# Float64 weight words to float32: two ScalarE passes and three VectorE passes in place of one and six

## The chip, the cores and the metric

The kernel runs on one core of one Trainium2 chip. The metric is the device time of one execution in microseconds. Engines: TensorE (PE, with PEld for its weight loads), VectorE (DVE), ScalarE (ACT), GpSimd (POOL) and SyncE (SP), which issues most DMAs.

## What is computed

Chunked attention, then a mixer. q, k and v have the shape (8, 8, 576, 64) in float32. In each chunk of 64 positions:

```python
scores = scale * np.matmul(q_c, k_c.transpose(0, 1, 2, 4, 3))
scores = scores - np.max(scores, axis=-1, keepdims=True)
attn = np.exp(scores)
attn = attn / (np.sum(attn, axis=-1, keepdims=True) + 1e-09)
out = np.matmul(attn, v_c)
```

With x of shape (8, 576, 512) made from the heads, the mixer is

```python
xt = x.transpose(0, 2, 1)
h = xt @ U @ V
u = x + h.transpose(0, 2, 1)
ch = np.maximum(u @ w_ch1, 0.0) @ w_ch2
return (u + ch).astype(np.float32)
```

U (576 x 32), V (32 x 576), w_ch1 (512 x 2048) and w_ch2 (2048 x 512) arrive as float64, since each is a float32 array times a float64 scalar. [...]

## The kernel before, in words

**Work.** Batches go in pairs; a pair is nine tiles of 128 positions (three groups of three). A tile's attention: q and k are transposed on TensorE (ps_qT, ps_kT) and copied by ScalarE, TensorE makes scores (sc), VectorE takes maxima and subtracts (mx, ex), ScalarE exponentiates (ex, L415), TensorE transposes (ps_eT), ScalarE copies (eT), TensorE multiplies by the values (av), VectorE divides (sm, x). A batch's x goes through U (xh and xl are its high and low parts, y, ys) and V (u), is added to x, transposed (ut) and split (uth, utl). Every float32 operand of a large product is split into a high part in float32r, which ScalarE casts, and a low part, which VectorE subtracts; a product is three matmuls. For each of 16 slices f of the hidden width, h (L567, 12 matmuls) is made, relu gives hh (ScalarE) and hl (VectorE), and o (L593, 9 matmuls for three tiles) is added up. Weights are read once, for the first pair, and stay.

**Weights.** A tile Wf holds 1024 values (512 of w_ch1, 512 of w_ch2) for each of 128 partitions. `w_ops` loads its raw words (wraw, stride two between high words and between low words), `rounding` makes float32 of them in wroom, `splitting` makes w: `high` is a ScalarE cast (L308), `low` a VectorE subtraction (L311). W13 to W15 are converted in halves. U (320 values) and V (144) go through the same `rounding`; V then makes a round trip through DRAM (vrows, vall) to be spread, and ScalarE's cast L256 and VectorE's L261 put it into vst.

**Conversion before.** ScalarE takes the absolute value of the high word as float32, times 2^16 (L86). VectorE: clamp (L92); shift left 4 and right 1, which drops the sign and makes room (L93); join the sign bit of the high word (L96); keep the exponent alone, into the high word (L99); multiply the low word by 2^-52 and that power of two (L100); add (L101).

**Order.** For the first pair the code makes a list of `Op`s, each with an engine, an estimated time, what it comes after, and what it takes and frees of the buffers. `order` runs through them as a planner with a clock of its own: of what can start next on an engine within 0.05 us it picks the lowest rank, and that fixes the order of every engine's instructions, DMA issues included. On the chip each engine then works in this order, and waits where something is late. `LEAD` gives the ranks of the first stage (tiles T, projections P, mixes M, U, V, W), `STRETCHES` the blocks of h, relu and o; TensorE's h has the lowest claim. `turn` chains the conversions: one begins after a given step of the one before. The later pairs have an order that is written out by hand and is not touched.

Of the kernel before, what the change touches and what calls it, by code (L numbers as in the profile page):

```python
# [10 lines left out]
F32 = mybir.dt.float32  # L11
F32R = mybir.dt.float32r
U32 = mybir.dt.uint32
AF = mybir.ActivationFunctionType
ALU = mybir.AluOpType
# [6 lines left out]
def kernel(  # L22
# [11 lines left out]
    nc = tc.nc  # L34
# [46 lines left out]

    def magnitude(raw, a):
        af = a.bitcast(F32)
        nc.scalar.activation(af, raw[..., 1].bitcast(F32), AF.Abs, scale=2.0**16)  # L86

    def as_f32(raw, a):
        hi, lo = raw[..., 1], raw[..., 0]
        af, hf = a.bitcast(F32), hi.bitcast(F32)  # L90
        return [
            lambda: nc.vector.tensor_scalar(af, af, HI_MIN, HI_MAX, op0=ALU.max, op1=ALU.min),  # L92
            lambda: nc.vector.tensor_scalar(  # L93
                a, a, 4, 1, op0=ALU.logical_shift_left, op1=ALU.logical_shift_right
            ),
            lambda: nc.vector.scalar_tensor_tensor(  # L96
                a, hi, 0x80000000, a, op0=ALU.bitwise_and, op1=ALU.bitwise_or
            ),
            lambda: nc.vector.tensor_scalar(hi, a, 0xFF800000, None, op0=ALU.bitwise_and),  # L99
            lambda: nc.vector.scalar_tensor_tensor(hf, lo, 2.0**-52, hf, op0=ALU.mult, op1=ALU.mult),  # L100
            lambda: nc.vector.tensor_add(af, af, hf),  # L101
        ]

    def wslot(shape, dtype, name):
        return wpool.tile([P, *shape], dtype, tag="w", name=name, bufs=NF)
# [68 lines left out]
    turn = [None]  # L174

    def rounding(raw, room, after, take, n):

        st = {}
        k = n / 1024

        def begin():
            st["a"] = room()
            magnitude(raw, st["a"])
            st["steps"] = as_f32(raw, st["a"])

        o = Op("ACT", 0.2 + 0.95 * k, begin, after, turn[0], take=take)
        for z in range(6):
            us = 0.15 + 0.54 * k if z in (0, 1, 3) else 0.15 + 1.07 * k
            o = Op("DVE", us, lambda z=z: st["steps"][z](), o)
            if z == 2:  # L190
                turn[0] = o
        return o, st

    def splitting(st, high, low, after, free, n):
        k = n / 1024
        h = Op("ACT", 0.2 + 0.85 * k, lambda: high(st["a"].bitcast(F32)), *after)
        return Op("DVE", 0.15 + 1.07 * k, lambda: low(st["a"].bitcast(F32)), h, free=free)

    def conversion(raw, room, high, low, after, take, free, n):
        o, st = rounding(raw, room, after, take, n)  # L200
        return splitting(st, high, low, [o], free, n)
# [30 lines left out]
    def v_ops():  # L232
# [29 lines left out]

        ld = Op("SP", 1.0, load, take="w", lat=2.0)
        o, _ = rounding(Later(lambda: st["raw"]), room, ld, "w", n)
        o = Op("SP", 0.6, join, o, free="w w", lat=2.5)
        o = Op("SP", 0.9, spread, o, take="w", lat=2.5)
# [13 lines left out]
    def w_ops(f, after=None):  # L280
# [15 lines left out]
        for z in range(n):  # L296
            cols = slice(z * size, (z + 1) * size)

            def room(z=z):
                return wslot((size,), U32, f"wroom_{f}") if n == 1 else slot(U32, f"wroom_{f}_{z}")  # L300

            def high(v, cols=cols):
                if cols.start == 0:
                    del st["raw"]
                    w = st["w"] = wslot((2, 2 * DM), F32R, f"w_{f}")
                    w1[f] = w[:, :, 0:DM].rearrange("p s (c f) -> p s c f", c=NCC)
                    w2[f] = w[:, :, DM:]
                nc.scalar.copy(st["w"][:, 0, cols], v)  # L308

            def low(v, cols=cols):  # L310
                nc.vector.tensor_sub(st["w"][:, 1, cols], v, st["w"][:, 0, cols])  # L311

            raw = Later(lambda cols=cols: st["raw"][:, cols])
            tag = "w" if n == 1 else "slot"
            halves.append((*rounding(raw, room, ld, tag, size), high, low, tag))
        rounded = [h[0] for h in halves]
        return [splitting(r, high, low, rounded, tag, size) for _, r, high, low, tag in halves]


# [337 lines left out]
    for item in LEAD.split():  # L657
        rank[0] += 1
        z, i = item[0], int(item[1:] or 0)
# [145 lines left out]
```

## Time and profile before

| | |
|---|---|
| runs, us | 1030.47, 1030.82, 1032.12 |
| median, us | 1030.82 |
| profiled execution, span, us | 1032.0 (the times have no figure of their own for it; the highest run is 0.12 us longer) |
| mean granted clock of TensorE | 0.929 |
| HBM read and written | 45.83 MB, 9.51 MB |

The page cuts the span into 40 slices of 25.8 us. A row of a timeline has the start, the duration, the engine, the line, the operation with output and input, the count, and in brackets the idle time before it with what ended it. A row of groups has the count, the busy time and the mean of one in ns, and behind the bar the idle time before. A row of windows has the stretch, then the busy time of PE, PEld, DVE, ACT and POOL with counts, then the granted clock, the DMA share and GB/s. Of a name such as wraw the buffer's number is left out in the profile.

### The profile page before, as it was taken

How to read it: one execution, taken by the hardware profiler on the slowest of the kernel's cores; microseconds unless marked ns; L12 is line 12 of the kernel's file. 1: busy time of each engine (PE TensorE's matmuls, PEld its weight loads, DVE VectorE, ACT ScalarE, POOL GpSimd, SP SyncE). 2: the span in 40 equal slices, each digit the busy share in tenths (PEclk: the TensorE clock that was granted, in tenths of full speed). 3: DMA queues.
4: the chain of work that ended last, by engine and by line, in shares of the span. 5: the costliest groups of instructions: out<-in, count | busy, mean ns of one | idle time of the engine just before them, and what ended most of it. 6: DMA issues, size and time to landing. Idle time of an engine off the chain costs nothing.

```text
span 1032.0 us, 16637 instructions
## 1 busy us (share of the span) xinstructions
PE 980.7 (95%) x7032; PEld 862.0 (84%) x7032; DVE 419.5 (41%) x834; ACT 260.8 (25%) x467; POOL 26.4 (3%) x78
## 2 busy tenths in 40 slices
PE   5486999999999999999999999999999999999998
PEld 4364888888888888988888888988888889999997
DVE  3498999973333342322423242322333332211211
ACT  3453234322322222222222222222222231111110
POOL 7100000000000000000000000000000000000000
PEclk9667899999999999999999999999999999999999
DMA  9952142305121211021021210111121000000000
GB/s 187 217 184 88 42 113 82 103 34 129 34 63 31 63 31 32 34 55 37 32 62 32 62 32 10 53 34 43 48 53 41 31 1 1 31 1 1 31 1 30
DMA packets 123157, 56.40 MB, mean 55 GB/s; under 512 B 107276, under 2 KB 115724, under 8 KB 123084
## 3 DMA queue, kind: packets, MB, share of 16 engines
q1 hardware_dynamic: 121932, 52.99, 20.1%
q0 software_dynamic: 1152, 2.36, 1.2%
q8 instruction: 55, 0.90, 0.4%
q14 instruction: 18, 0.15, 0.0%
HBM read 45.83 MB, written 9.51 MB: 54 GB/s over the span
## 4 chain that ended last, share of the span: by engine, by line
PE 69%; DVE 0%; ACT 0%; DVEq 0%; issue 0%; ACTq 0%
PE h L567 30%; PE o L593 30%; PE av L424 1%; PE sc L393 1%; PE ut L535 1%; PE ps_eT L375 1%; PE ps_kT L375 1%; PE ps_qT L375 1%; PE u L523 1%; PE y L496 1%; PE y L495 1%; DVE x L605 0%; DVE ex L411 0%; ACT ex L415 0%; DVEq L800 0%; DVE mx L407 0%
## 5 line engine op out<-in xcount | busy, mean ns | idle before, releaser
L567 PE MATMUL h<-uth,w 128*128 128x384 f32 x1536 | 427.1, 342 | 4.9 <-ACT w L308 2.1
L593 PE MATMUL o<-w,hh 128*128 128x512 f32 x1152 | 364.3, 403 | 0.6 <-ACT hh L575 0.6
L567 PEld LDWEIGHTS h<-uth,w 128*128 128x128 f32 x1536 | 282.4, 189 | 13.8 <-ACT w L308 2.6
L580 DVE SCALAR_TENSOR_TENSOR hl<-h,hh 128x384 fp32r<-128x384 f32 x192 | 106.8, 556 | 430.4 <-ACT hh L575 430.4
L567 PE MATMUL h<-utl,w 128*128 128x384 f32 x768 | 260.2, 339 | 0.4 <-DVE utl L548 0.4
L593 PEld LDWEIGHTS o<-w,hh 128*128 128x128 f32 x1152 | 207.8, 189 | 35.8 <-ACT hh L575 0.9
L593 PE MATMUL o<-w,hl 128*128 128x512 f32 x576 | 217.9, 395 | 0.0
L575 ACT ACTIVATE hh<-h 128x384 fp32r<-128x384 f32 x192 | 94.3, 491 | 477.3 <-PE h L567 477.2
L567 PEld LDWEIGHTS h<-utl,w 128*128 128x128 f32 x768 | 144.9, 189 | 6.6 <-DVE utl L548 0.6
L593 PEld LDWEIGHTS o<-w,hl 128*128 128x128 f32 x576 | 108.2, 188 | 25.0 <-DVE hl L580 0.3
L375 PE MATMUL ps_eT<-ident,ex 128*128 128x128 f32 x144 | 24.8, 301 | 25.0 <-ACT ex L415 25.0
L415 ACT ACTIVATE ex<-ex 128x512 f32<-128x512 f32 x36 | 22.7, 632 | 89.7 <-DVE ex L411 89.1
L375 PEld LDWEIGHTS ps_eT<-ident,ex 128*128 128x128 f32 x144 | 18.9, 153 | 31.1 <-ACT ex L415 27.9
L407 DVE TENSOR_REDUCE mx<-sc 128x4 f32<-128x256 f32 x72 | 28.0, 418 | 37.7 <-PE sc L393 37.7
L488 DVE TENSOR_TENSOR xl<-x,xh 128x512 fp32r<-128x512 f32 x40 | 27.2, 687 | 29.6 <-ACT xh L484 25.6
L529 DVE TENSOR_TENSOR x<-u,x 128x512 f32<-128x512 f32 x36 | 24.1, 684 | 26.7 <-PE u L523 26.4
L548 DVE TENSOR_TENSOR utl<-ut,uth 128x512 fp32r<-128x512 f32 x36 | 24.5, 690 | 25.2 <-ACT uth L543 25.1
L605 DVE TENSOR_TENSOR x<-o,x 128x512 f32<-128x512 f32 x48 | 31.2, 685 | 7.7 <-PE o L593 7.6
L543 ACT CAST uth<-ut 128x512 fp32r<-128x512 f32 x36 | 20.9, 587 | 40.4 <-PE ut L535 36.6
L385 ACT COPY eT<-ps_eT 128x512 f32<-128x512 f32 x36 | 21.1, 586 | 39.4 <-PE ps_eT L375 39.4
L484 ACT CAST xh<-x 128x512 fp32r<-128x512 f32 x40 | 24.1, 621 | 17.8 <-PE y L496 7.5
L411 DVE TENSOR_TENSOR ex<-sc,mx 128x256 f32<-128x256 f32 x72 | 28.0, 417 | 0.8
(74 smaller groups left out, 590.2 us busy)
## 6 DMA issues: line engine op xcount, KB each, us to landing
wraw<-in_moe_w_ch_dram SPq DMA_DIRECT2D x32, 512.0 KB, 4.5
out_dram<-x SPq DMA_DIRECT2D x36, 256.0 KB, 2.1
vn<-in_v_dram SPq DMA_DIRECT2D x108, 64.0 KB, 2.9
qn<-in_q_dram SPq DMA_DIRECT2D x24, 256.0 KB, 3.3
kn<-in_k_dram SPq DMA_DIRECT2D x24, 256.0 KB, 4.1
qkv<-in_v_dram POOLq DMA_DIRECT2D x36, 64.0 KB, 6.3
qkv<-in_q_dram SPq DMA_DIRECT2D x8, 256.0 KB, 9.4
qkv<-in_k_dram SPq DMA_DIRECT2D x8, 256.0 KB, 7.6
```

The costliest lines, as they stand in the source:

```text
L375: nc.tensor.transpose(ps[:, j * P : (j + 1) * P], src[:, j * P : (j + 1) * P], ident)
L407: nc.vector.reduce_max(mx, st["sc"][e], axis=AX.X)
L411: nc.vector.tensor_sub(st["ex"][:, :, e, :], st["sc"][e], mx.unsqueeze(2).broadcast_to([P, HP, C]))
L484: nc.scalar.copy(st["h"], x_of[pr, i + 4 * e])
L488: nc.vector.tensor_sub(st["l"], x_of[pr, i + 4 * e], st["h"])
L529: nc.vector.tensor_add(x, st["u"], x)
L548: nc.vector.tensor_sub(ul[:, :, js], st["t"].rearrange("p (c t) -> p c t", c=NCC), uh[:, :, js])
L567: nc.tensor.matmul(ps[:, :GN], lhsT=w[:, z, cc], rhs=u[:, cc, :], start=(n == 0), stop=(n == 3 * NCC - 1))
L575: nc.scalar.activation(hh, ps[:, :GN], AF.Relu)
L580: nc.vector.scalar_tensor_tensor(hl, ps[:, :GN], 0.0, hh, op0=ALU.max, op1=ALU.subtract)
L593: nc.tensor.matmul(acc[j], lhsT=h[:, js], rhs=w2[f][:, z], start=(first and i == 0), stop=(final and i == 2),)
L605: nc.vector.tensor_add(x, ps, x)
```

## The change

`as_f32` now has three VectorE steps. The clamp stays (its line is 96 now). ScalarE gets a second pass, `low_bits` (line 90): the low word, as an integer, times 0.9375 x 2^-29 x (1 - 2^-10), in place and back to an integer, so that three bits of it remain, rounded. VectorE ors the high word's sign into it (line 97), then shifts the clamped word left by 3 and ors the low word in (line 100). The result is joined from bits, where before it was added from two floats. `rounding` makes the plan of these: the second pass `b` comes after the first on ScalarE, the sign join waits for both, and the next conversion may begin after the clamp (`turn`), where it was the third VectorE step. Every line behind moves down by 7.

```diff
+    LOW_STEP = 0.9375 * 2.0**-29 * (1.0 - 2.0**-10)
+
     def magnitude(raw, a):
-        af = a.bitcast(F32)
-        nc.scalar.activation(af, raw[..., 1].bitcast(F32), AF.Abs, scale=2.0**16)
+        nc.scalar.activation(a.bitcast(F32), raw[..., 1].bitcast(F32), AF.Abs, scale=2.0**16)
+
+    def low_bits(raw):
+        nc.scalar.activation(raw[..., 0], raw[..., 0], AF.Copy, scale=LOW_STEP)
...
             lambda: nc.vector.tensor_scalar(af, af, HI_MIN, HI_MAX, op0=ALU.max, op1=ALU.min),
-            lambda: nc.vector.tensor_scalar(
-                a, a, 4, 1, op0=ALU.logical_shift_left, op1=ALU.logical_shift_right
+            lambda: nc.vector.scalar_tensor_tensor(
+                lo, hi, 0x80000000, lo, op0=ALU.bitwise_and, op1=ALU.bitwise_or
             ),
             lambda: nc.vector.scalar_tensor_tensor(
-                a, hi, 0x80000000, a, op0=ALU.bitwise_and, op1=ALU.bitwise_or
+                a, a, 3, lo, op0=ALU.logical_shift_left, op1=ALU.bitwise_or
             ),
-            lambda: nc.vector.tensor_scalar(hi, a, 0xFF800000, None, op0=ALU.bitwise_and),
-            lambda: nc.vector.scalar_tensor_tensor(hf, lo, 2.0**-52, hf, op0=ALU.mult, op1=ALU.mult),
-            lambda: nc.vector.tensor_add(af, af, hf),
         ]
...
         o = Op("ACT", 0.2 + 0.95 * k, begin, after, turn[0], take=take)
-        for z in range(6):
-            us = 0.15 + 0.54 * k if z in (0, 1, 3) else 0.15 + 1.07 * k
-            o = Op("DVE", us, lambda z=z: st["steps"][z](), o)
-            if z == 2:
-                turn[0] = o
+        b = Op("ACT", 0.2 + 0.95 * k, lambda: low_bits(raw_of(raw)), o)
+        o = Op("DVE", 0.15 + 0.54 * k, lambda: st["steps"][0](), o)
+        turn[0] = o
+        o = Op("DVE", 0.15 + 1.07 * k, lambda: st["steps"][1](), o, b)
+        o = Op("DVE", 0.15 + 1.07 * k, lambda: st["steps"][2](), o)
         return o, st
```

Since the planner's times and chains change, the order moves on all engines in the first pair. SyncE's DMA issues are the same up to the loads of the second pair's first tile. Three places follow; wraw_249 is W0, wraw_346 and wraw_347 are W1, wraw_517 is W2, and the number behind a name is a buffer's.

ScalarE around V's cast (vst), before:

```order
L385 COPY eT_3_475<-ps_eT_3_445 128x512
L256 CAST vst<-vall 128x576
L484 CAST xh_0_3_526<-x_3_520 128x512
L415 ACTIVATE ex_4_501<-ex_4_501 128x512
L385 COPY qkT_5_542<-ps_qT_5_528 128x512
L385 COPY qkT_5_542<-ps_kT_5_535 128x512
L385 COPY eT_4_557<-ps_eT_4_544 128x512
L86 ACTIVATE wroom_583<-wraw_347 128x1024
```

and now:

```order
L392 COPY eT_3_472<-ps_eT_3_444 128x512
L87 ACTIVATE wroom_480<-wraw_346 128x1024
L90 ACTIVATE wraw_346<-wraw_346 128x1024
L422 ACTIVATE ex_4_500<-ex_4_500 128x512
L263 CAST vst<-vall 128x576
L491 CAST xh_0_3_533<-x_3_523 128x512
L392 COPY eT_4_540<-ps_eT_4_528 128x512
L392 COPY qkT_5_553<-ps_qT_5_535 128x512
```

W1's passes and the exponential of tile 4 have moved ahead of the cast that waits for V, and the eT copy of tile 4 ahead of tile 5's copies.

VectorE at the same place, W0's steps, before:

```order
L261 TENSOR_TENSOR vst<-vall,vst 32x576
L488 TENSOR_TENSOR xl_0_3_540<-x_3_520,xh_0_3_526 128x512
L93 TENSOR_SCALAR wroom_410<-wroom_410 128x1024
L96 SCALAR_TENSOR_TENSOR wroom_410<-wraw_249,wroom_410 128x1024
L99 TENSOR_SCALAR wraw_249<-wroom_410 128x1024
L100 SCALAR_TENSOR_TENSOR wraw_249<-wraw_249 128x1024
```

and now:

```order
L97 SCALAR_TENSOR_TENSOR wraw_249<-wraw_249 128x1024
L495 TENSOR_TENSOR xl_0_3_542<-x_3_523,xh_0_3_533 128x512
L268 TENSOR_TENSOR vst<-vall,vst 32x576
L100 SCALAR_TENSOR_TENSOR wroom_406<-wroom_406,wraw_249 128x1024
L443 TENSOR_SCALAR sm_4_582<-av_0_4_556 128x4
```

The first of W0's two joins stands ahead of vst, the second right behind it.

VectorE ahead of the exponential of tile 8, before:

```order
L605 TENSOR_TENSOR x_2_437<-o_2_914,x_2_437 128x512
L442 TENSOR_TENSOR x_7_951<-av_0_7_926,sm_7_947 128x4x64
L100 SCALAR_TENSOR_TENSOR wraw_517<-wraw_517 128x1024
L101 TENSOR_TENSOR wroom_710<-wroom_710,wraw_517 128x1024
L407 TENSOR_REDUCE mx_8_964<-sc_0_8_888 128x4
L411 TENSOR_TENSOR ex_8_963<-sc_0_8_888,mx_8_964 128x4x64
L407 TENSOR_REDUCE mx_8_964<-sc_0_8_889 128x4
L311 TENSOR_TENSOR w_966<-wroom_710,w_966 128x1024
L411 TENSOR_TENSOR ex_8_963<-sc_0_8_889,mx_8_964 128x4x64
```

and now:

```order
L612 TENSOR_TENSOR x_0_261<-o_0_887,x_0_261 128x512
L612 TENSOR_TENSOR x_1_336<-o_1_906,x_1_336 128x512
L612 TENSOR_TENSOR x_2_433<-o_2_915,x_2_433 128x512
L449 TENSOR_TENSOR x_7_960<-av_0_7_924,sm_7_947 128x4x64
L449 TENSOR_TENSOR x_7_960<-av_0_7_925,sm_7_947 128x4x64
L418 TENSOR_TENSOR ex_8_919<-sc_0_8_869,mx_8_920 128x4x64
```

W2's last passes and three of tile 8's four steps have moved ahead of the adds of o.

More of the change, by code (lines that the diff above doesn't have):

```diff
@@ L80 @@
     w2 = {}
+    LOW_STEP = 0.9375 * 2.0**-29 * (1.0 - 2.0**-10)
     def magnitude(raw, a):
-        af = a.bitcast(F32)
-        nc.scalar.activation(af, raw[..., 1].bitcast(F32), AF.Abs, scale=2.0**16)
+        nc.scalar.activation(a.bitcast(F32), raw[..., 1].bitcast(F32), AF.Abs, scale=2.0**16)
+    def low_bits(raw):
+        nc.scalar.activation(raw[..., 0], raw[..., 0], AF.Copy, scale=LOW_STEP)
     def as_f32(raw, a):
         hi, lo = raw[..., 1], raw[..., 0]
-        af, hf = a.bitcast(F32), hi.bitcast(F32)
+        af = a.bitcast(F32)
         return [
             lambda: nc.vector.tensor_scalar(af, af, HI_MIN, HI_MAX, op0=ALU.max, op1=ALU.min),
-            lambda: nc.vector.tensor_scalar(
-                a, a, 4, 1, op0=ALU.logical_shift_left, op1=ALU.logical_shift_right
+            lambda: nc.vector.scalar_tensor_tensor(
+                lo, hi, 0x80000000, lo, op0=ALU.bitwise_and, op1=ALU.bitwise_or
             ),
             lambda: nc.vector.scalar_tensor_tensor(
-                a, hi, 0x80000000, a, op0=ALU.bitwise_and, op1=ALU.bitwise_or
+                a, a, 3, lo, op0=ALU.logical_shift_left, op1=ALU.bitwise_or
             ),
-            lambda: nc.vector.tensor_scalar(hi, a, 0xFF800000, None, op0=ALU.bitwise_and),
-            lambda: nc.vector.scalar_tensor_tensor(hf, lo, 2.0**-52, hf, op0=ALU.mult, op1=ALU.mult),
-            lambda: nc.vector.tensor_add(af, af, hf),
         ]
@@ L197, in splitting, with raw_of @@
         return Op("DVE", 0.15 + 1.07 * k, lambda: low(st["a"].bitcast(F32)), h, free=free)
+    def raw_of(raw):
+        return raw.get() if isinstance(raw, Later) else raw
     def conversion(raw, room, high, low, after, take, free, n):
```

## The prediction

> **What bounds the kernel now.** I read the page first: busy shares, and the 40 slices (25.8 us each) for where TensorE is not busy.
>
> ```profile
> PE 980.7 (95%) x7032; PEld 862.0 (84%) x7032; DVE 419.5 (41%) x834; ACT 260.8 (25%) x467; POOL 26.4 (3%) x78
> PE   5486999999999999999999999999999999999998
> DVE  3498999973333342322423242322333332211211
> PEclk9667899999999999999999999999999999999999
> ```
>
> TensorE is busy for 980.7 of 1032.0 us, so 51.3 us are idle, and the row of slices puts nearly all of them into the first four slices, where the granted clock is low too. VectorE's row has its nines in slices 4 to 7, so it is full where TensorE is not. From the fifth slice on, only TensorE's own work counts, and the change leaves that alone. So I asked the chain of waits for TensorE over the first 150 us, and then its timeline for the places.
>
> ```profile
> PE ps_eT L375 <- ACT ex L415: 24.5, 3, 10.4
> PE u L523 <- DVE ys L506: 3.0, 2, 1.6
> ...
> 49.96 1.12 PE L375 MATMUL ps_eT<-ident,ex 128*128 128x128 f32 x4 [10.45 <-ACT ex L415]
> 59.81 1.65 PE L523 MATMUL u<-ys,vst 128*128 128x512 f32 x3 [1.62 <-DVE ys L506]
> 72.23 0.45 PE L567 MATMUL h<-uth,w 128*128 128x384 f32 x1 [1.67 <-ACT w L308]
> 73.49 1.01 PE L567 MATMUL h<-uth,w 128*128 128x384 f32 x2 [0.63 <-DVE w L311]
> 92.14 1.12 PE L375 MATMUL ps_eT<-ident,ex 128*128 128x128 f32 x4 [6.90 <-ACT ex L415]
> 146.14 0.44 PE L567 MATMUL h<-uth,w 128*128 128x384 f32 x1 [0.46 <-ACT w L308]
> 147.52 0.61 PE L567 MATMUL h<-uth,w 128*128 128x384 f32 x2 [0.76 <-DVE w L311]
> ```
>
> The reader sees five places. The first (10.45 us) and a similar one of 7 us near 22 us are not VectorE's: ScalarE itself stood still there for V's float64 words and for their way through DRAM.
>
> ```profile
> 28.05 0.33 ACT L86 ACTIVATE vroom<-vraw 128x144 f32<-128x144 f32 x1 [7.60 <-DMA vraw<-in_moe_V_dram]
> 48.18 0.67 ACT L256 CAST vst<-vall 128x576 fp32r<-128x576 f32 x1 [11.61 <-DMA vall<-vrows]
> ```
>
> The queue of SyncE is the same in both kernels beyond these transfers, so both landings stay: up to 48.18 us I credit nothing. The other places wait on conversions of weights that VectorE does in order with the attention's small steps.
>
> **The change part by part.** The price of one of each pass, from the groups kept apart by shape, first 130 us:
>
> ```profile
> L86 ACT ACTIVATE wroom<-wraw 128x1024 f32<-128x1024 f32 x7 | 8.1, 1152 | 0.0
> L100 DVE SCALAR_TENSOR_TENSOR wraw<-wraw 128x1024 f32<-128x1024 uint32 x6 | 7.3, 1221 | 0.1
> L96 DVE SCALAR_TENSOR_TENSOR wroom<-wraw,wroom 128x1024 uint32<-128x1024 uint32 x6 | 7.3, 1220 | 0.1
> L101 DVE TENSOR_TENSOR wroom<-wroom,wraw 128x1024 f32<-128x1024 f32 x6 | 7.3, 1220 | 0.1
> L308 ACT CAST w<-wroom 128x1024 fp32r<-128x1024 f32 x6 | 6.3, 1051 | 8.4 <-DVE wroom L101 8.4
> L92 DVE TENSOR_SCALAR wroom<-wroom 128x1024 f32<-128x1024 f32 x7 | 5.0, 712 | 0.0
> L93 DVE TENSOR_SCALAR wroom<-wroom 128x1024 uint32<-128x1024 uint32 x7 | 4.8, 690 | 0.1
> L99 DVE TENSOR_SCALAR wraw<-wroom 128x1024 uint32<-128x1024 uint32 x6 | 4.1, 689 | 0.1
> ```
>
> A weight tile costs VectorE 0.71 + 0.69 + 1.22 + 0.69 + 1.22 + 1.22 = 5.75 us before, and 0.71 + 1.22 + 1.22 = 3.15 us now, if the two new joins cost what the two old scalar_tensor_tensor rows cost; they read and write the same strided words as L96 and L100. That is 2.6 us less for each of 16 tiles, 41.6 us in all. It buys time only at the places above. ScalarE pays one more pass. The trace has none that writes uint32 at stride two; nearest are L86 (1152 ns, strided read) and L308 (1051 ns). I take 1.15 us; the floor is 1.05, and I set the ceiling at twice L86, 2.3 us, for a strided read and write together. Over 16 tiles that is about 18 us (17 to 37) on an engine that is busy 25% of the time.
>
> The Trainium skill, page "ScalarE: Activation LUTs", section "Rules for kernel authors", speaks against such a move: it says to run multiplications on VectorE, not on ScalarE. By instruction the rows agree (1152 ns against 689 to 712 for a VectorE pass over one tensor), and the sum over busy time would be a loss by that rule; the sum below goes by who waits.
>
> Place by place, with TensorE's own times:
>
> *u at 59.81.* Between V's arrival and ys, VectorE runs without a break.
>
> ```profile
> 48.89 0.75 DVE L261 TENSOR_TENSOR vst<-vall,vst 32x576 fp32r<-32x576 f32 x1 [8.91 <-ACT vst L256]
> ...
> 51.86 1.22 PE L424 MATMUL av<-qkv,eT 64*64 64x65 f32 x31
> ...
> 55.30 1.21 DVE L101 TENSOR_TENSOR wroom<-wroom,wraw 128x1024 f32<-128x1024 f32 x1
> ...
> 59.07 0.68 DVE L506 TENSOR_TENSOR ys<-y,ys 32x512 fp32r<-32x512 f32 x1
> ```
>
> From L93 to L101 (ending at 56.5) five passes of tile W0 stand there: 0.69 + 1.22 + 0.69 + 1.22 + 1.22 = 5.04 us. In the new order the sign join stands ahead of vst, in the 8.91 us in which VectorE idles, so one pass of 1.22 remains: 3.8 us less. That is the ceiling. What is late next is the chain from tile 4's values (av, 51.86) over x, its split and y to ys. The new order puts exp, transpose and eT of tile 4 around the wait for V, so av can start when the eT copy ends: V's cast at 48.18, one split and one copy of about 0.6 each, 49.9 us, 2.0 us sooner than 51.86. Between 2.0 and 3.8 I take 2.3, near the chain. W1's two ScalarE passes now stand ahead of exp of tile 4 and of V's cast; W1 landed by 32.28 + 7.2 = 39.5 us at the latest,
>
> ```profile
> 32.28 1.59 SPq L289 DMA_DIRECT2D wraw<-in_moe_w_ch_dram  x1
> DMA to landing us min/median/max: 4.9/6.1/7.2
> ```
>
> so with exp they end near 39.5 + 1.15 + 1.15 + 0.6 = 42.4, 5.8 us ahead of V; even at the ceiling they cost nothing.
>
> *h of W1 at 72.23 and 73.49.* The waits are 1.67 + 0.63 = 2.30 us, both on W1. VectorE spends 2.6 us less on W1 and starts on it 2.3 us sooner, so W1 is ready ahead of its h and this wait goes. Next is exp of tile 6, whose transpose the new order puts ahead of W1's h on TensorE. VectorE comes to its four steps (0.42 us each) while h of W0 still runs; they and exp (0.63) are 2.3 us, of which I put 0.7 under h of W0, so that 1.6 us of wait remain. That leaves 2.30 - 1.6 = 0.7. Beside it, two products take 1.01 us at 73.49 and 0.61 at 147.52: the clock is at half there, for a stretch of about 3 us that costs some 1.3, and whether it comes again is open. 0.7 to 2.0; I take 1.5.
>
> *eT of tile 8 at 92.14.* Here is the longest stretch.
>
> ```profile
> 84.57 1.39 DVE L605 TENSOR_TENSOR x<-o,x 128x512 f32<-128x512 f32 x2
> 85.88 0.41 DVE L442 TENSOR_TENSOR x<-av,sm 128x256 f32<-128x256 f32 x1
> 86.21 1.22 DVE L100 SCALAR_TENSOR_TENSOR wraw<-wraw 128x1024 f32<-128x1024 uint32 x1
> ...
> 90.94 0.42 DVE L411 TENSOR_TENSOR ex<-sc,mx 128x256 f32<-128x256 f32 x1
> 91.46 0.63 ACT L415 ACTIVATE ex<-ex 128x512 f32<-128x512 f32 x1 [1.69 <-DVE ex L411]
> ```
>
> From 86.21 to 90.94 VectorE does L100 and L101 of W2, three steps of tile 8, and the low part of W2. In the new order all of that stands ahead of the last out-adds. What follows the last o on VectorE is one add (half of 1.39), two halves of x (0.41 each), one subtraction (0.42); then exp (0.63): with the hops about 2.6 us. 6.90 - 2.6 = 4.3 us gained. If tile 8's steps slipped back behind, three of 0.4 us each return: 3.1 is the floor, 4.3 I take.
>
> *ys of batch 1.* ScalarE's queue now has both passes of W4 ahead of the ys cast, which TensorE awaits for u; before, L86 came behind it.
>
> ```profile
> 100.59 0.58 ACT L505 CAST ys<-y 128x512 fp32r<-128x512 f32 x1 [1.40 <-PE y L496]
> ```
>
> ScalarE had 1.40 us of idle time there, and the two passes are 2.3 us: a loss of 0.9, from 0 (the passes begin sooner) to 1.15 + 2.3 - 1.4 = 2.0 at the ceiling. This is the one wait that the change adds on the path.
>
> *W7 at 146.* 0.46 + 0.76 = 1.2 us, both on conversions; VectorE has shed 2.6 us for each of W3 to W7 by then. It goes: 1.2, floor 0.
>
> Sum: 2.3 + 1.5 + 4.3 - 0.9 + 1.2 = 8.4 us. The profiled execution's span is 1032.0; the median of the runs is 1030.82, 0.11% less. 1032.0 - 8.4 = 1023.6 in its terms, 1022.4 in the median's. With every floor the sum is 2.0 + 0.7 + 3.1 - 2.0 + 0 = 3.8, with every ceiling 3.8 + 2.0 + 4.3 - 0 + 1.2 = 11.3.
>
> **The rivals.** *The clock keeps up.* The granted clock (the column after POOL's) around the 1.62 us wait at 59.81 and behind the waits of 1.67 and 0.63:
>
> ```profile
> 56.00:58.00 2.00, 1.26 (x34) 0.95 (x34) 1.97 (x5) 2.00 (x4) 0.00 (x0) 0.95 0.68 239
> 64.00:66.00 2.00, 2.00 (x27) 1.67 (x30) 2.00 (x3) 1.73 (x3) 0.00 (x0) 0.50 0.00 0
> 74.00:76.00 2.00, 2.00 (x8) 2.00 (x7) 1.93 (x6) 0.63 (x1) 0.00 (x0) 0.50 0.66 177
> ```
>
> It fell from 0.95 to 0.50 behind so short a wait and was still there at 66 us. I reckon with the same after the new, shorter waits of some 0.7, 1.6 and 2.6 us. If these leave the clock at 0.95, the half-clock stretches behind 59.81, 73.49 and 92.14 go: 6 us the first, and I put 3 on each of the others, 12 us of work that takes 6 at full clock; with two thirds of that on TensorE's own path it is 4 us: 1022.4 - 4 = 1018.4. Against it speak the rows. The Trainium skill, page "TensorE: Matmul & The Clock Gate", section "Why this matters for your kernels", says that idle gaps up to about 3 us do not drop the clock; the trace disagrees here at 1.62 us. 12%.
>
> *No gain.* VectorE is freed, but each place finds another late partner (y's chain, exp, ys): TensorE's waits keep their length and move to other releasers. For it: ScalarE and VectorE hand work to each other at every place. Against: the 6.90 us have VectorE's passes in them and nothing else. Time 1030.8. 8%.
>
> *Slower: relu behind the second pass.* From W4 to W15 each second pass stands in ScalarE's queue close to a relu that TensorE needs.
>
> ```profile
> 114.20 0.49 ACT L575 ACTIVATE hh<-h 128x384 fp32r<-128x384 f32 x1 [1.62 <-PE h L567]
> 116.09 0.62 PE L593 MATMUL o<-w,hh 128*128 128x512 f32 x2
> ```
>
> That relu ends 1.4 us before its o starts. A pass of 1.15 us in front fits, one of 2.3 does not: 0.9 us exposed, 12 times, 10.8 us, 1022.4 + 10.8 = 1033.2. It decides the sign from an exposure of 8.4 / 12 = 0.7 us on, so at a pass of 2.1 us. Against it: ScalarE's two rows of 1024 words lie at 1.05 and 1.15. 8%.
>
> **How the numbers follow.** Forecast 72%, clock 12%, no gain 8%, slower 8%. The time is the forecast's, 1022.4. Its own terms span 1030.82 - 11.3 = 1019.5 to 1030.82 - 3.8 = 1027.0; the clock rival reaches to 1018, and with three quarters of the 6 us and the ceilings it goes below 1017. I give 1016.5 to 1027.5: what lies above is the two other rivals, 16%. About 0.2%, 2.1 us, is what a measurement of this kernel can tell from no change. Faster: 72 + 12 = 84%; same 8%; slower 8%.
>
> **What would show it.** Right: VectorE's busy time near 419.5 - 42 - 2 (U, V) = 376, ScalarE's near 260.8 + 19 = 280; V's cast still near 48.2 us, with TensorE idle for some 9 us ahead of it; the wait before eT of tile 8 at 2 to 3 us, with W2's passes ahead of it; no wait on w near 146; from there on the same gaps as before. Wrong: a second pass of 2 us or more; waits of o on hh in the chain of waits; a TensorE wait for ys over 3 us; u of the first three tiles starting no sooner than 59 us.

## The result and the profile after

The changed kernel takes 1019.45 us (median of 4 runs, 1018.70 to 1019.85), the kernel before in the same session 1031.47 us (1030.47 to 1032.59): a ratio of 0.9877 with a 95% interval of 0.9863 to 0.9890, 12.0 us faster. The forecast was 8.4 us and 1022.4 us. The profiled execution after took 1019.85 us and has a span of 1018.0 us, so 1.85 us lie around a span. Before's profiled span, 1032.0 us, is thus 2.4 us above what its median gives (1031.47 - 1.85 = 1029.6): at its end the two profiles are 14.0 us apart, and some 2 of these belong to the two executions and not to the change.

The page's busy times and three rows of slices (now of 25.45 us):

```profile
PE 974.4 (96%) x7032; PEld 856.4 (84%) x7032; DVE 375.6 (37%) x771; ACT 277.8 (27%) x488; POOL 26.4 (3%) x78
PE   5487999999999999999999999999999999999998
DVE  3398995233333333223323332322323232211211
PEclk9689999999999999999999999999999999999999
```

VectorE's 375.6 and ScalarE's 277.8 us are the forecast's 376 and 280. In the row of the granted clock slices 3 to 5 have 8, 9, 9 where they had 6, 7, 8. The prices, from the groups of the first 130 us kept apart by shape:

```profile
L87 ACT ACTIVATE wroom<-wraw 128x1024 f32<-128x1024 f32 x11 | 12.7, 1154 | 3.6 <-DMA wraw<-in_moe_w_ch_dram 3.6
L90 ACT ACTIVATE wraw<-wraw 128x1024 uint32<-128x1024 uint32 x11 | 12.6, 1147 | 0.0
L100 DVE SCALAR_TENSOR_TENSOR wroom<-wroom,wraw 128x1024 uint32<-128x1024 uint32 x10 | 12.2, 1220 | 0.2
L97 DVE SCALAR_TENSOR_TENSOR wraw<-wraw 128x1024 uint32<-128x1024 uint32 x10 | 12.2, 1219 | 0.0
L96 DVE TENSOR_SCALAR wroom<-wroom 128x1024 f32<-128x1024 f32 x10 | 6.9, 685 | 0.0
```

The new ScalarE pass (L90) costs 1.147 us, where 1.15 was taken; the joins cost 1.22 us as their forerunners did. The count is the second thing to see: 11 first passes lie in these 130 us where before had 7, so the conversions run ahead. The chain of waits for TensorE, first 150 us:

```profile
PE ps_eT L382 <- ACT ex L422: 14.4, 4, 7.8
...
PE av L431 <- issue: 4.7, 2, 4.5
...
PE u L530 <- DVE ys L513: 2.5, 2, 2.0
```

The waits for exponentials fell from 24.5 to 14.4 us. The 4.5 us in front of av are the wait for V, which stood elsewhere before. Of h there is no wait on w left: W1's and W7's are gone. The places, from TensorE's timeline:

```profile
50.93 1.26 PE L431 MATMUL av<-qkv,eT 64*64 64x65 f32 x32 [4.49 <-issue]
58.14 0.96 PE L530 MATMUL u<-ys,vst 128*128 128x512 f32 x3 [0.51 <-DVE ys L513]
69.59 1.01 PE L382 MATMUL ps_eT<-ident,ex 128*128 128x128 f32 x4 [2.17 <-ACT ex L422]
84.66 0.50 PE L503 MATMUL y<-xl,ust 128*128 128x512 f32 x1 [2.15 <-DVE xl L495]
85.00 0.63 PE L382 MATMUL ps_eT<-ident,ex 128*128 128x128 f32 x4
90.31 0.50 PE L503 MATMUL y<-xl,ust 128*128 128x512 f32 x1 [0.36 <-DVE xl L495]
92.81 2.24 PE L530 MATMUL u<-ys,vst 128*128 128x512 f32 x6 [2.00 <-DVE ys L513]
99.30 0.44 PE L574 MATMUL h<-uth,w 128*128 128x384 f32 x1 [0.73 <-ACT uth L550]
```

Against before, the first u (59.81) is 1.7 us sooner, the transposes of tile 8 (92.14) 7.1, the last low product of y and h of the second block 9.7:

```profile
100.05 0.50 PE L496 MATMUL y<-xl,ust 128*128 128x512 f32 x1 [0.31 <-DVE xl L488]
...
109.01 0.45 PE L567 MATMUL h<-uth,w 128*128 128x384 f32 x1 [0.71 <-ACT uth L543]
```

So 2.6 us came between tile 8's transposes and that y. The durations there tell most of it: the four transposes take 1.12 us before and 0.63 after. The work there is not quite the same: before has five pairs of products y behind the transposes, after four, since one pair is done ahead of them (its low product stands at 84.66). In stretches of 40, 50 and 130 us, of before (after the length: busy time of PE, PEld, DVE, ACT, POOL, then the granted clock, the DMA share, GB/s):

```profile
60.00:100.00 40.00, 29.19 (x295) 22.75 (x295) 34.46 (x68) 16.40 (x26) 0.12 (x1) 0.76 0.33 111
100.00:150.00 50.00, 46.23 (x222) 40.58 (x223) 47.12 (x59) 17.58 (x24) 0.00 (x0) 0.89 0.21 71
130.00:260.00 130.00, 126.85 (x787) 112.06 (x786) 100.50 (x156) 43.13 (x71) 0.45 (x4) 0.95 0.32 92
```

and of after:

```profile
60.00:100.00 40.00, 29.79 (x316) 22.87 (x316) 36.13 (x70) 23.35 (x35) 0.11 (x1) 0.91 0.34 112
100.00:150.00 50.00, 49.86 (x251) 45.28 (x252) 47.84 (x59) 32.31 (x40) 0.00 (x0) 1.00 0.40 133
130.00:260.00 130.00, 129.09 (x862) 114.27 (x861) 61.00 (x111) 43.11 (x75) 0.57 (x5) 1.00 0.30 80
```

The granted clock's mean rises from 0.76 to 0.91 and from 0.89 to 1.00. (Undisturbed, that execution of before shows 0.95 and after shows 1.00; the same matmul of h takes 0.34 us in both, so this difference is not 5% of speed.) From 130 to 260 us TensorE is idle for 0.91 us where it was for 3.15: 2.24 us more. 9.7 and 2.2 are 11.9 us.

The two profiles are 14.0 us apart, and what is left lies behind h of the second block. From it to one relu (ScalarE; it starts at 268.66 us before and at 255.83 after, 12.8 apart) TensorE does the same 991 instructions in both, and beside the idle time its busy time falls by 0.9 us (156.11 to 155.22). The filled kernel at tile 8 (below), in the old order, has 156.05, so this belongs to the order; what in it gives the 0.9 us, the traces don't show. From this relu to the last one (1023.22 and 1009.27) the same 5234 instructions take 754.0 us of TensorE before and 752.9 after; in the filled kernel, which has a clock of 1.00, they take 753.0. These 1.1 us go with the lower granted clock of that one execution of before (0.95) and are no work of the change. So the parts below are those of 12.8 us in these two executions, and the medians are 12.0 apart: 0.8 us of the parts are the luck of the two.

### The profile page after: what moved, and what is told of

It is laid out like the page before. It is cut to its first block, busy times and chain, and to the rows that moved or that the text cites. A ratio compares the mean times of both kernels' runs of the same rounds, so it can differ in the third digit from the quotient of the medians.

```text
span 1018.0 us, 16610 instructions
## 1 busy us (share of the span) xinstructions
PE 974.4 (96%) x7032; PEld 856.4 (84%) x7032; DVE 375.6 (37%) x771; ACT 277.8 (27%) x488; POOL 26.4 (3%) x78
## 4 chain that ended last, share of the span: by engine, by line
PE 70%; DVE 0%; ACT 0%; DVEq 0%; issue 0%; ACTq 0%
PE h L574 31%; PE o L600 31%; PE av L431 1%; PE sc L400 1%; PE ut L542 1%; PE ps_eT L382 1%; PE ps_kT L382 1%; PE ps_qT L382 1%; PE u L530 1%; PE y L503 1%; PE y L502 1%; DVE x L612 0%; DVE ex L418 0%; ACT ex L422 0%; DVEq L807 0%; DVE mx L414 0%
```

## The experiments

The theory behind the prediction: VectorE's passes stand in front of the attention's small steps, so fewer of them shorten TensorE's waits, while the pass added on ScalarE is hidden. Each experiment changes one part of after; one (the clock behind tile 8) starts from before. The times of before, measured on the same chip, are 1032.77 us (new order with old passes, old order with new passes, third pass, shift on VectorE), 1032.64 (`turn`, V early, old passes from W4, filled waits) and 1032.43 (the three on the clock). Two medians of one kernel differed by up to 1.3 us from chip to chip, so ratios are compared.

**The passes alone.** The new passes in the old order: the planner is given the six VectorE steps and their times, and three of them do nothing on the chip. ScalarE's two passes stand together at the place of the one.

```diff
-        b = Op("ACT", 0.2 + 0.95 * k, lambda: low_bits(raw_of(raw)), o)
-        o = Op("DVE", 0.15 + 0.54 * k, lambda: st["steps"][0](), o)
+            low_bits(raw)
+            st["steps"] = as_f32(raw, st["a"]) + [lambda: None] * 3
...
+        for z in range(6):
+            us = 0.15 + 0.54 * k if z in (0, 1, 3) else 0.15 + 1.07 * k
```

> The order of before with the new arithmetic: both ScalarE passes at the place of the first, the three VectorE steps at the places of the first three, nothing at the last three. Theory (fewer passes): VectorE's busy time near 376 us, the wait ahead of tile 8's exponential falls from 6.9 to some 4.5 us (2.4 us of passes gone), the waits on W1 go: 1021 to 1025 us. Rival (the order): 1028 to 1031 us.

1025.34 us (1024.42 to 1026.88), ratio 0.9932 (0.9916 to 0.9948): 7.4 us of gain, just above the theory's range and clear of the rival's.

```profile
87.89 1.11 PE L380 MATMUL ps_eT<-ident,ex 128*128 128x128 f32 x4 [5.08 <-ACT ex L420]
...
104.84 0.45 PE L572 MATMUL h<-uth,w 128*128 128x384 f32 x1 [0.72 <-ACT uth L548]
```

The wait ahead of tile 8 is 5.08 us (the theory had some 4.5), between 6.90 (before) and 2.15 (after), and behind it the transposes still run at half clock (1.11 us). The passes alone bring some 6 tenths of the gain, the order made from their new times the other 5 us.

**The order alone.** The changed order with the old arithmetic: the six old VectorE instructions at the places of the three new ones, and nothing in place of the second ScalarE pass.

```diff
     def low_bits(raw):
-        nc.scalar.activation(raw[..., 0], raw[..., 0], AF.Copy, scale=LOW_STEP)
+        pass
...
+            sign,
+            lows,
```

> The changed kernel's order with the old arithmetic: at the place of the second step stand the old shift and sign join, at the place of the third the old exponent, multiply and add; ScalarE's second pass isn't issued. Theory (fewer VectorE passes carry the gain): VectorE's busy time is back near 419 us, the wait ahead of the exponential of tile 8 is over 4 us again, and most of the 12 us is lost: 1026 to 1031 us. Rival (the new order carries the gain, by filling the wait for V and by moving W2 ahead of tile 8): 1019 to 1023 us.

1058.32 us (1057.55 to 1060.42), ratio 1.0253 (1.0235 to 1.0271): some 26 us slower than before, outside both expectations. What o waits for, from TensorE's waits of the first 200 us:

```profile
PE o L606 <- DVE hl L593: 8.2, 7, 2.5
PE o L606 <- ACT hh L588: 5.5, 3, 2.0
```

H of the second block in its timeline:

```profile
106.85 0.44 PE L580 MATMUL h<-uth,w 128*128 128x384 f32 x1 [0.72 <-ACT uth L556]
```

And three stretches of 26 us behind it (columns as above):

```profile
104.00:130.00 26.00, 20.68 (x87) 17.55 (x87) 24.71 (x29) 7.59 (x10) 0.00 (x0) 0.84 0.27 96
130.00:156.00 26.00, 22.93 (x104) 18.89 (x103) 25.57 (x31) 9.57 (x12) 0.00 (x0) 0.93 0.23 82
156.00:182.00 26.00, 19.57 (x82) 16.67 (x81) 25.43 (x34) 7.66 (x12) 0.00 (x0) 0.87 0.41 121
```

At h of the second block this kernel is 2.2 us ahead of before (106.85 against 109.01); from there to the end it loses some 28 us. VectorE is busy for 75.7 of 78 us, and o waits for hl, which VectorE makes behind the conversions that the order has pulled forward. The order is no gain by itself: it spends the time that the new passes save.

**Where that loss lies.** The same, but with the new passes for U, V and W0 to W3, and the old ones from W4 on.

```diff
+    OLD = lambda f: f >= 4
...
-            st["steps"] = as_f32(raw, st["a"])
+            st["steps"] = (as_f32_old if old else as_f32)(raw, st["a"])
...
+        b = Op("ACT", 0.2 + 0.95 * k, lambda: None if old else low_bits(raw_of(raw)), o)
```

> The changed kernel's order; U, V and W0 to W3 by the new passes, W4 to W15 by the old ones at the places of the new steps. The run with all old passes in this order had h of group 1 at 106.85 us against 99.30 in the changed kernel and lost the rest behind it, with VectorE busy 95 to 98% from 104 to 182 us and o waiting for hl. Theory (with the new order the later tiles are what cannot bear old passes, since relu's low part sits behind them): h of group 1 near 99 us, and still a loss behind it: 1040 to 1052 us. Rival (what hurts is the early tiles; with these quick, the later ones hide): 1020 to 1028 us.

1050.87 us (1048.98 to 1053.23), ratio 1.0180 (1.0159 to 1.0202), as the theory had it.

```profile
98.76 0.69 PE L598 MATMUL h<-uth,w 128*128 128x384 f32 x1 [0.67 <-ACT uth L574]
113.77 0.73 PE L624 MATMUL o<-w,hh 128*128 128x512 f32 x2 [1.98 <-ACT hh L606]
...
168.14 0.50 PE L624 MATMUL o<-w,hl 128*128 128x512 f32 x1 [2.56 <-DVE hl L611]
```

H of the second block comes at 98.76 us, as in after, and the 31 us against after lie behind it; the largest waits of TensorE from there to 260 us are those of o on hl and hh, 13.3 us in all. The gain up to 99 us is that of W0 to W3; the later tiles must be light so that the order can keep it.

**Is ScalarE's pass hidden?** The first ScalarE pass is done twice; the planner does not know of it.

```diff
             magnitude(raw, st["a"])
+            magnitude(raw, st["a"])
```

> The changed kernel with ScalarE's first pass done twice, its order kept: ScalarE has 1.15 us more for each weight tile, VectorE the same. Theory (ScalarE has room; only the ys cast of batch 1 and one or two other places sit behind its passes): 1020 to 1023 us, ScalarE's busy time near 297 us. Rival (relu queues behind the passes): waits of o on hh appear, 12 tiles by up to 1.1 us: 1026 to 1033 us.

1021.26 us (1019.31 to 1022.79), ratio 0.9890 (0.9869 to 0.9911). With 18 us more on ScalarE (296.2 us) the median is 1.8 us above after's, as the theory had it, though the two intervals overlap. The trace shows the pass at one place, ys of the second batch:

```profile
69.31 0.65 PE L383 MATMUL ps_eT<-ident,ex 128*128 128x128 f32 x4 [2.16 <-ACT ex L423]
...
92.31 2.93 PE L531 MATMUL u<-ys,vst 128*128 128x512 f32 x6 [3.04 <-DVE ys L514]
```

The wait for ys rose from 2.00 to 3.04 us, by one pass. This execution (1019.83 us, the second fastest of four) still ends where after's does (spans of 1018.1 and 1018.0), because it was 1.5 us ahead there, mainly since the clock stayed up at tile 6: its transposes take 0.65 us here and 1.01 in after behind a wait of the same length. No wait of o on hh came. Two passes more than before, 2.3 us in all, are what the prediction's ceiling put on ScalarE; here they cost at most this, and not the 10.8 us of the slower rival.

**The third pass on VectorE.** In place of the second ScalarE pass VectorE shifts the low word right by 29 (three bits of it, cut off and not rounded).

```diff
-        nc.scalar.activation(raw[..., 0], raw[..., 0], AF.Copy, scale=LOW_STEP)
+        nc.vector.tensor_scalar(raw[..., 0], raw[..., 0], 29, None, op0=ALU.logical_shift_right)
```

> The second ScalarE pass is taken out; a VectorE shift right by 29 (0.69 us for a weight tile) makes the three low bits, cut off, not rounded. ScalarE has one pass as before the change, VectorE four in place of six; the planner knows. Theory: half-way by VectorE's work (minus 1.9 us for each tile in place of 2.6), and ys of batch 1 no longer waits for two passes: 1018 to 1022 us. Rival (what matters is that VectorE gave its work to ScalarE): a quarter of the gain goes, 1021 to 1024 us.

1023.79 us (1023.15 to 1026.81), ratio 0.9922 (0.9899 to 0.9946), in the rival's range; VectorE 386.2, ScalarE 261.1 us. By engine time it would be cheaper (10.6 us more on VectorE against 16.7 less on ScalarE), and it is some 4 us slower. H of the second block comes at 101.49 us, 2.2 later than in after. The planner made another order of it too, so the 4 us are those of the pass and its order together. The Trainium skill's rule for multiplications (page "ScalarE: Activation LUTs", section "Rules for kernel authors") would put such a pass on VectorE; here the measurement, pass and order together, speaks the other way. The theory's reason is that VectorE is the engine that stands in front of TensorE's waits.

**Two details of the plan.** Let the next conversion begin after the third VectorE step, as before, and not after the clamp; or rank V ahead of U and tile 2.

```diff
         o = Op("DVE", 0.15 + 0.54 * k, lambda: st["steps"][0](), o)
-        turn[0] = o
...
         o = Op("DVE", 0.15 + 1.07 * k, lambda: st["steps"][2](), o)
+        turn[0] = o
```

> The changed kernel, planned with the next conversion allowed to begin after the third VectorE step of the one before, as it was before, in place of after the clamp. Theory (VectorE's passes carry the gain, the rule of turn is a detail): 1018 to 1022 us. Rival (starting the next tile's ScalarE passes ahead of V's wait is what gains): 1023 to 1026 us, with W0's steps behind V's cast again.

1020.55 us (1019.92 to 1021.81), ratio 0.9887 (0.9869 to 0.9905), as the theory had it.

```diff
-    LEAD = "T0 T1 U T2 T3 T4 P0 V W0 M0 T5 ...
+    LEAD = "T0 T1 V U T2 T3 T4 P0 W0 M0 T5 ...
```

> The changed kernel with V moved to the third place of the leading list, ahead of U, so that its words are loaded, converted and sent through DRAM before tiles 2 to 4. Theory (7.8 us and most of 5.6 us of ScalarE's idle time, and with it some 16 us of TensorE's waits up to 51 us, are V's landing and not conversions): these waits go, u of the first tiles starts 4 to 8 us sooner: 1011 to 1016 us. Rival (all transfers together bound the first 50 us, DMA share near 1): TensorE waits for q and k instead: 1017 to 1021 us.

1021.26 us (1020.13 to 1021.49), ratio 0.9889 (0.9872 to 0.9906): the theory's 1011 to 1016 us did not come, though V's cast came at 35.90 us in place of 49.15. In the first the long wait for V stands ahead of tile 4's transposes again (10.26 us) and u comes at 61.01 us, 2.9 later than in after; in the second it has moved to tile 2:

```profile
37.15 1.12 PE L382 MATMUL ps_eT<-ident,ex 128*128 128x128 f32 x4 [12.81 <-ACT ex L422]
```

In both, h of the second block stands at 99.5 us (99.47 and 99.52), as in after (99.30). What is won or lost before 60 us is caught up by then. That the chain of VectorE and ScalarE sets the pace there fits this, but was not tested by itself.

**The clock ahead of 60 us.** After, with 48, 32 and 32 idle transposes of the identity in the waits ahead of tile 2's and tile 4's transposes and of av of tile 4.

```diff
+            for j in range({("eT_", 0, 2): 48, ("eT_", 0, 4): 32}.get((name, pr, t), 0)):
+                nc.tensor.transpose(ps[:, 0:P], ident, ident)
...
+            for j in range(32 if (pr, t) == (0, 4) else 0):
+                nc.tensor.transpose(ps[0][:, 0:P], ident, ident)
```

> The changed kernel with idle transposes of the identity on TensorE in the three long waits ahead of 51 us (48 ahead of eT of tile 2, 32 ahead of eT of tile 4, 32 ahead of the values of tile 4), into banks that are written over behind. Nothing else is moved. Theory (the half clock behind long waits costs TensorE's path): the half-clock time falls from 32 us to under 15, and the stretch from 51 to 57 us gets shorter: 1016.5 to 1018.5 us. Rival (the chain there is bound by ScalarE and VectorE, or the extra work delays): 1019 to 1021 us.

1019.41 us (1018.63 to 1020.56), ratio 0.9875 (0.9858 to 0.9893): nothing, as the rival had it. The half-clock time from 25 to 60 us fell from 23.9 us (the theory had counted 32) to 6.8, the mean granted clock from 28 to 60 us rose from 0.67 to 0.89, and yet av of tile 4 came at 51.21 us (after: 50.93). TensorE is not what is waited for there.

**The clock behind tile 8, in the kernel before.** 38 idle transposes ahead of tile 8's, in the wait of 6.90 us; all else is before.

```diff
+            for j in range({("eT_", 0, 8): 38}.get((name, pr, t), 0)):
+                nc.tensor.transpose(ps[:, 0:P], ident, ident)
```

> The kernel before, with 38 idle transposes of the identity in front of the transposes of tile 8's exponential, in the wait of 6.90 us there (four take 0.63 us at full clock, so 38 take some 6.0). Theory: of what the change gained between that place (7.1 us ahead) and the last low product of y (9.7 us ahead), 2.6 us came from a clock that stayed up behind a shorter wait. Then this kernel has them without the change: the transposes of tile 8 still start near 92.1 us, the low product of y near 97.5 in place of 100.05, h of the second block near 106.4 in place of 109.0, and the time is 1028.9 against 1031.5. Rival: those 2.6 us came from work that was put in another order, and the clock is worth nothing here; then the time stays at 1031.5, within 0.5.

1030.43 us (median of 12, 1028.36 to 1033.03) against 1032.43, ratio 0.9980 (0.9969 to 0.9990): 2.0 us faster (1.0 to 3.2), by work that is thrown away.

```profile
90.26 0.66 PE L377 MATMUL ps_eT<-ident,ex 128*128 128x128 f32 x4 [2.77 <-ACT ex L417]
...
96.02 0.50 PE L498 MATMUL y<-xl,ust 128*128 128x512 f32 x1 [0.30 <-DVE xl L490]
```

From tile 8's transposes to the last y are 5.76 us here, 7.91 before (92.14 to 100.05) and 5.31 in after. The granted clock from 92 to 96 us is 1.00, in before 0.50. The work there is the same as in before, so 2.15 of the 2.6 us were the clock and the theory holds. The 0.45 left against after are the rival's, the order of work: they are the pair of products y that after does ahead of the transposes, and such a pair takes 0.46 us here. That tile 8 came at 90.26 and not at 92.1 is not the filler's doing: this execution, the fastest of the 12, was 1.9 us ahead at the last o in front of the filler (82.94 against 84.84), 1.4 of them since h of W1, where the clock stayed up (two products in 0.61 us, before in 1.01).

**The same in the other direction.** After, with each of tile 8's two subtractions done six times over: ten more instructions on VectorE.

```diff
+            for _ in range(6 if (pr, t) == (0, 8) else 1):
                 nc.vector.tensor_sub(st["ex"][:, :, e, :], st["sc"][e], mx.unsqueeze(2).broadcast_to([P, HP, C]))
```

> The changed kernel, with each of the two subtractions of tile 8 done six times over (same result; ten more VectorE instructions of about 0.41 us, 4.1 us ahead of that tile's exponential). Theory: the wait of 2.15 us near 82.5 becomes one of about 6, the granted clock falls to a half behind it as it did before the change, and the loss is the 4.1 us and some 2.6 us more: h of the second block near 106 in place of 99.3, the time near 1026. Rival: the clock costs nothing, the loss is the delay alone: h of the second block near 103.4, 1023.6.

1024.82 us (1023.57 to 1025.45), ratio 0.9925 (0.9913 to 0.9937): 5.0 us in the span (1023.0 against 1018.0), between the rival's 4.1 and the theory's 6.7. H of the second block comes at 104.08 us, where the theory had 106 and the rival 103.4.

```profile
88.21 0.80 PE L504 MATMUL y<-xl,ust 128*128 128x512 f32 x1 [4.81 <-DVE xl L496]
88.80 1.06 PE L382 MATMUL ps_eT<-ident,ex 128*128 128x128 f32 x4
...
95.32 0.50 PE L504 MATMUL y<-xl,ust 128*128 128x512 f32 x1 [0.36 <-DVE xl L496]
```

The granted clock behind the wait is the number after POOL's:

```profile
88.00:92.00 4.00, 3.79 (x41) 2.78 (x41) 2.56 (x5) 0.80 (x2) 0.11 (x1) 0.57 0.00 0
```

The first low y is 3.55 us later than in after (88.21 against 84.66), and from there to the last y it takes 7.11 us in place of 5.65: 1.46 more, at half clock. So the clock did fall behind the longer wait, of 4.81 us, but for less time: a mean of 0.57 over 4 us is 4 x 0.43 / 0.50 = 3.4 us at half clock, and the wait of 6.90 us had 6.8 by the same reckoning. The theory's mechanism is there, its size was too large.

**The clock at tile 6.** After, with 14 idle transposes ahead of tile 6's, and 14 ahead of u of tile 3.

```diff
+            for j in range({("eT_", 0, 6): 14}.get((name, pr, t), 0)):
+                nc.tensor.transpose(ps[:, 0:P], ident, ident)
...
+            for j in range(14 if (pr, t) == (0, 3) else 0):
+                nc.tensor.transpose(ps[:, 0:P], ident, ident)
```

> The changed kernel with 14 idle transposes (2.2 us at full clock) in the wait of 2.17 us for the exponential of tile 6, and 14 in the wait of 2.00 us for ys of the second batch. Theory: the half-clock stretches of 68 to 72 and 92 to 96 us go; the four groups of TensorE behind the first wait take 4.17 us now and would take 2.5, and the six products u behind the second 2.24 and would take some 1.5: 2.4 us, the time near 1017.1. Rival: what TensorE waits for next is bound by VectorE and ScalarE, as it was in the first 50 us, and nothing is gained: 1019.4.

1019.78 us (1018.95 to 1020.48), ratio 0.9881 (0.9866 to 0.9895): no gain that can be told.

```profile
69.76 0.60 PE L384 MATMUL ps_eT<-ident,ex 128*128 128x128 f32 x4
...
83.21 0.50 PE L505 MATMUL y<-xl,ust 128*128 128x512 f32 x1 [2.14 <-DVE xl L497]
...
91.32 2.92 PE L534 MATMUL u<-ys,vst 128*128 128x512 f32 x6 [1.95 <-DVE ys L515]
...
98.29 0.44 PE L578 MATMUL h<-uth,w 128*128 128x384 f32 x1 [0.72 <-ACT uth L554]
```

The first half did its part: tile 6's transposes take 0.60 us in place of 1.01, and y is 1.45 us sooner (83.21 against 84.66). The second missed its place, since u of tile 3 is made near 65 us and the wait for ys stands ahead of another tile: there the clock fell again, and u took 2.92 us (2.24 in after). At 98.29 us 1.0 us of lead is left, in one execution; the medians do not show it. Whether a filler at the right place would gain 1 us stays open.

## Why the prediction was right, and where not

The direction, the range and the mechanism held; the likeliest time was 3 us too high (a gain of 12.0 us for 8.4), mainly because a rival of 12%, the clock that keeps up, came true at two of its three places. The forecast's own terms reached down to 1019.5 us: the measured 1019.45 lies at their edge, and it is inside the range because that was widened for the clock.

Three readings in the prediction are wrong, without harm to the sum. VectorE's nines stand in slices 3 and 5 to 8, while TensorE is idle in slices 1 to 4; the two rows do not show that VectorE is full where TensorE is not, and the waits had to show it. The sum over busy time was never a loss: VectorE gave up 43.9 us and ScalarE took on 17.0. And W1 had not landed by 39.5 us: ScalarE waited for it until 40.87 in after, which V's cast at 49.15 hid.

By the steps of the sum:

- **u at 59.81**, forecast 2.3 us: it is 1.7 us sooner by start. V's cast came at 49.15 us where 48.18 was taken, by the DMA; against that cast it is 2.6. av came 50.93 - 49.15 = 1.8 us behind the cast, as worked out (49.9 - 48.18 = 1.7).
- **h of W1**, forecast 1.5 us: nothing. The waits on W1 went, and the wait for tile 6's exponential that takes their place is 2.17 us and not 1.6. The step that failed is the cover: VectorE has the low part of W1 (1.22 us) in front of tile 6's four steps.

```profile
66.08 1.22 DVE L318 TENSOR_TENSOR w<-wroom,w 128x1024 fp32r<-128x1024 f32 x1
67.21 0.42 DVE L414 TENSOR_REDUCE mx<-sc 128x4 f32<-128x256 f32 x1
...
68.45 0.42 DVE L418 TENSOR_TENSOR ex<-sc,mx 128x256 f32<-128x256 f32 x1
```

  The four steps end at 68.87 us, 1.4 us after h of W0 (67.43). I had put 0.7 us of them under it; only the first had begun. The clock fell to a half behind this wait, too, as it had before.
- **eT of tile 8**, forecast 4.3 us: the wait fell from 6.90 to 2.15 us, 4.75, and the start gained 7.1 - 2.95 = 4.2 against the last o (84.84 and 81.89). Right in place, partner (the adds of o, x, one subtraction) and size.
- **ys of batch 1**, forecast a loss of 0.9 us: the wait grew from 1.39 to 2.00, a loss of 0.6. Right; the third ScalarE pass lengthened this wait and no other by a pass.
- **W7**, forecast 1.2 us: no wait on w is left near 146 us, and 2.2 us less idle time lies between 130 and 260. Mis-sized: I counted the one place and not the ones behind it.
- **What no term held**: the clock. Behind u at 58.14 it stayed up (three products in 0.96 us, before in 1.65), and h of W0 was 2.5 us sooner where u was 1.7; behind the wait ahead of tile 8 it stayed up, and of the 2.6 us there 2.15 are shown to be the clock by the filled wait; from u of the second batch to h it gave 0.6 (u in 2.24 us, before in 2.93). I had chosen half clock behind every wait, from the rows behind 59.81 and 73.49. These are 3.5 us, and the rival had 4; the 0.8 and the 0.6 are read from durations and no run tested them alone. The Trainium skill (page "TensorE: Matmul & The Clock Gate", section "Why this matters for your kernels") says to leave no idle gap over about 3 us, or the clock drops. That gaps below it are harmless does not follow in this trace: the clock stayed up behind the wait of 2.15 us, and not behind the one of 2.17.

These add up: 1.7 + 0 + 4.2 - 0.6 + 2.2 = 7.5 us for the five terms (forecast 8.4), 0.8 + 2.15 + 0.6 = 3.5 for the clock and 0.5 for the pair of y done ahead, together 11.5. What is left of 11.9, some 0.5, is what TensorE gained on the way to the last o: h of W1 and the transposes and scores around it are done at 77.96 us before (the first o follows) and at 75.47 after (av follows), 2.5 us apart, and the last o is 2.95 apart. What gave it is not settled, and neither is what gave the 0.9 us of busy time behind h of the second block.

Of the rivals, "no gain" fell with the first timeline; it is true for the first 50 us alone, where waits moved and nothing was won. "Slower, relu behind the second pass" fell: no wait of o on hh came, not even with a third pass of the same length. What would have made a kernel slower was none of my rivals: an order planned for light conversions that meets heavy ones (1058 us).

## What to carry to other kernels

Do not price a pass that is moved by the engines' busy time: find the waits of the bounding engine, and count what stands in front of each on the releasing engine. Where an order is planned from estimated times, test passes and order apart: here the passes alone gave 7 us, the order alone cost 26, and both together gave 12: the order is right only with the passes that it was planned for. And a wait that gets shorter can pay twice if the clock behind it stays up; fill the wait with idle matmuls in the old kernel to see how much of a gain that is.

## What the runs showed of the hardware

- Behind a wait of 2.15 us near 82.5 us the clock stayed at its full value, behind one of 2.17 us near 67.4 it fell to a half (transposes of 1.01 us for 0.63), in the same execution; behind 1.62 us it had fallen in before, and behind 2.77 us (tile 8 in the filled kernel) it stayed up. The length of the wait alone does not decide. What else does can be read from the traces: in all 13 of them the granted clock changes only after whole multiples of 3.41 us, on a grid that lies anew in each execution. The same wait at tile 6, in after (first two rows) and with the third ScalarE pass (last two), cut at that grid:

```profile
66.33:69.74 3.41, 1.25 (x8) 0.93 (x7) 3.34 (x7) 1.38 (x3) 0.00 (x0) 1.00 0.36 145
69.74:73.15 3.41, 3.41 (x44) 2.96 (x43) 3.34 (x6) 2.12 (x4) 0.00 (x0) 0.50 0.09 17
...
65.51:68.92 3.41, 1.64 (x10) 1.32 (x8) 3.34 (x8) 1.11 (x3) 0.00 (x0) 1.00 0.41 162
68.92:72.33 3.41, 3.02 (x50) 2.79 (x50) 2.97 (x4) 3.38 (x6) 0.00 (x0) 1.00 0.12 25
```

  In after the wait of 2.17 us lies within one stretch: TensorE is busy for 1.25 of its 3.41 us (37%), and the next stretch has half clock. With the third pass the wait of 2.16 us reaches across the edge at 68.92: 1.64 us (48%) are busy ahead of it, and the clock stays. In the 13 traces, from the first clock record (near 20 us) to 130 us, full clock was always lost behind a stretch with under 48% busy and always kept behind one with over 57%; at half clock it never came back behind one with under 81%. These are what the traces show, not limits that a run looked for. So a wait of about 2 us can cost a stretch at half clock in one execution and not in the next.
- 32 to 48 idle transposes in a wait raised the mean granted clock (from 0.67 to 0.89 from 28 to 60 us in after, and from 0.50 to 1.00 from 92 to 96 in before). That was worth nothing where TensorE is not the one waited for (0.0 us ahead of 60 us), and 2.0 us where its own work follows.
- A granted clock of 0.95 in place of 1.00 went with 1.1 us more in 754 (the same 5234 instructions of TensorE), 0.15% and not 5%.
- ScalarE's pass from uint32 to uint32, in place and at stride two, takes 1147 ns for 1024 values, no more than its float pass with a strided read alone (1154 ns). VectorE's clamp is as fast after (685 ns) as before: the mean of 712 ns there has one instruction of 0.88 us among seven, and the others take 0.68 to 0.69.
